# Linear attention and a gated convolution: the output product in 64x64 quadrants, with a new written-out order

## The chip, the core and the metric

The kernel runs on one core of a Trainium2 chip. TensorE (PE; PEld is its weight load) multiplies, VectorE (DVE) and ScalarE (ACT) do the elementwise work and empty the accumulator tiles, GpSimd (POOL) starts the loads, SyncE (SP) starts the stores. The metric is the device time of one execution in microseconds (us); lower is better. Beside the runs there is one profiled execution, whose span goes from its first to its last instruction.

## The reference

For each of 8 batches and 8 heads of dimension 64, over a sequence of 576: `kv = k^T v` (64x64), `out = q kv`, then a root-mean-square norm along the head dimension with a gain. The heads side by side make rows of 512, and these go through a gated convolution layer:

```python
kv = np.einsum('bhsd,bhse->bhde', k, v)
out = np.einsum('bhsd,bhde->bhse', q, kv)
rms = np.sqrt(np.mean(out * out, axis=-1, keepdims=True) + 1e-06)
x = out / rms * g_norm                     # heads side by side: 576 x 512 per batch
h = np.maximum(x @ w_in, 0.0)              # 576 x 1024
conv_out = sum(conv_w[k] * shifted(h, k - 1) for k in range(3))
y = (h * sigmoid(conv_out)) @ w_out        # 576 x 512
```

Inputs and outputs are fp32; the kernel computes in bf16 with fp32 accumulation.

## The kernel before, in words

Everything is unrolled. Small functions (`ops`) each emit a few instructions; the string ORDER lists their calls one after the other, and at the end of the kernel each engine is bound to issue its instructions in exactly that order. A token such as `ot.4.1@1` calls `ot(4, 1)` with accumulator slot 1; `!A` or `!V` gives an eviction to ACT or DVE. There are four accumulator slots in PSUM (`a0` to `a3`, each 128 x 1024 fp32), two buffers each for q, k and v, and four output row buffers.

The names that matter here, with b for the batch and lines of the kernel before:

- `Lq`, `Lk`, `Lv` (lines 310 to 320), `Li`, `Lo`: loads, which cast fp32 to bf16 on the way, all started by POOL in order. A batch's q lies as [128, 4, 576]: a row of partitions holds heads 2w and 2w+1 of slot w in its halves, each with 64 groups of 9 rows. Batch 0's first half comes through a staging tile instead (`pre`, `ca`).
- `qt` (line 372): 36 transposes of 64x64 blocks for two head pairs, `qc` copies them out as `qT`. `kv` (line 344): 36 (or 72) matmuls of 64x64x64 for k^T v. Both use one quarter (quadrant) of the 128x128 array per instruction: `half[v]` chooses the rows, `half[c]` the columns.
- `kvc` (line 355): copies k^T v into `kvbd`, one 128x128 block-diagonal tile per head pair, whose other quarters were zeroed once at the start (lines 260 and 263). Each copy fills one partition half.
- `ot` (line 387): output product of one head pair t; full-width matmuls of 128x128 by 64 and by 512 columns (`mm576`, line 382) with `kvbd` as weights.
- Norm, batches 0 and 1: `sq` (square, ACT), `on` (sums by a matmul with ones), `nl` (reciprocal root, ACT), `mz` (gain and scale, DVE). Batches 2 to 7 in pairs: `sq` and `oc` (copy, both ACT), `ss`, `ln`, `sl`, then `sp` (spreads the scale into PSUM, PE) and `mu` (gain and scale, DVE).
- Layer: `hm` (lines 474 to 481, 288 columns) or `ha`, `hb` (lines 488 to 509, 512 and 128 columns) are x times w_in; `re`, `rea`, `reb` the relu; `ta`, `aa`, `ab` the three taps on DVE; `sg` the sigmoid on ACT; `mg` the product with the gate on DVE; `om` (line 558) times w_out, `ea` empties it, `st` stores.
- `fi` and `fo` (lines 277 to 285): fillers, matmuls of zeros that keep TensorE running while it would wait.

The output product of the kernel before and the copy that feeds it:

```python
    def kvc(b, u, i=None, eng=None):
        if b not in HALF:
            u, i = None, u
        ps = T["kvps", b, u][half[i]]
        to = kvbd[b % 2][half[i], :, half[i]].rearrange("p (u v) e -> p u v e", u=2)
    ...
    def ot(b, t):
        mm576(tl(("ot", b, t), "a", [P, 1024], FP32, "o_ps"), kvbd[b % 2][:, t, :], T["qT", b, t // 2][:, t % 2, :])
```

Of the kernel before, what the change touches and what calls it, by code (L numbers as in the profile page):

```python
# [59 lines left out]
HALF = [0, 1]  # L60
CONV = {0: (0, 1), 1: (1, 1), 2: (2, 2), 3: (4, 2), 4: (6, 1), 5: (7, 1)}
# [18 lines left out]
sg.0.7 fi.1.512@1 fi.1.128@1 qt.3.1@1 hm.1.7.1 hm.1.6.0@2 sg.0.6 qc.3.1!V@4 aa.0.0 re.1.7!A re.0.4!A hm.1.6.1  # L80
hm.1.3.0@1 re.1.6!A ab.0.0 qt.3.0@3 hm.1.2.0@0 hm.1.2.1 mg.0.3 ta.0.4@1 qc.3.0!A@0 sg.0.0 hm.1.3.1 kv.3@2 hm.1.5.0@3
re.1.2!A sg.0.1 ta.0.5 aa.0.2 hm.1.5.1 hm.1.1.0@0 ab.0.2 re.1.3!A kvc.3.0!A mg.0.0 sg.0.4 kvc.3.1!A Lo.1 hm.1.0.0@1
hm.1.0.1 re.1.0!A sg.0.5 ta.1.3@0 hm.1.1.1 ta.1.2 re.1.1!A qt.2.0@2 re.1.5!V qt.2.1@1 Lk.2@1 ot.3.1@3 sq.3.1@0
oc.3.1@4 aa.1.1 Lv.2@1 qc.2.1!V@1 ot.3.0@0 oc.3.0 mg.0.2 ab.1.1 ot.3.3@1 fi.2.128@3 om.0.1.1@3 oc.3.3@0 sq.3.0@1
ta.1.1@1 sg.1.2 ot.3.2@0 Lo.0 sq.3.3@2 sq.3.2@3 qc.2.0!V@2 ta.1.0 aa.1.0 oc.3.2 ab.1.0 hm.1.4.0@2 hm.1.4.1 sg.1.3
Lq.5@0 fi.3.128@1 kv.2@1 om.0.0.1@0 kvc.2.0!V kvc.2.1!V sg.1.0 re.1.4!A ot.2.3@1 mg.1.1 sg.1.1 ta.1.5@0 ot.2.0@2
ta.1.4 sq.2.3@4 oc.2.3@1 oc.2.0@2 sq.2.0@5 mg.1.0 ta.1.7@1 om.0.1.0 ot.2.1@1 aa.1.2 ab.1.2 oc.2.1 om.0.0.0 sq.2.1@6
Lq.4@1 Lv.4@0 sg.1.5 ta.1.6 ea.0.0!A@0 aa.1.3 ot.2.2@2 sg.1.4 ab.1.3 sg.1.7 om.0.3.0@1 sg.1.6 om.0.2.0@0 ea.0.1!V@1
mg.1.2 mg.1.3 sq.2.2@7 Lk.4@0 ss.2@3 ss.3 oc.2.2 ln.1@0 om.0.2.1 Lv.5@1 Lk.5@1 qt.5.1@2 st.0.0 sl.1@0 qt.5.0@3
ea.0.2!A@2 om.0.3.1 sp.3.0.1@0 qc.5.1!V@3 mu.3.0.1@1 sp.2.1.0@2 qc.5.0!A@0 ea.0.3!A@3 mu.2.1.0 kv.4@3 sp.3.0.0@1  # L90
mu.3.0.0 Lq.6@0 kvc.4.0!A kvc.4.1!A qt.4.1@0 qc.4.1!A@4 sp.3.1.1@3 om.0.4.0@2 sp.3.1.0@1 sp.2.0.0@0 st.0.1 mu.3.1.1
mu.3.1.0 qt.4.0@3 om.0.4.1 mu.2.0.0 qc.4.0!A@2 sp.2.1.1@1 ea.0.4!A@0 mu.2.1.1 kv.5@0 kvc.5.1!A sp.2.0.1@3 ot.4.1@1
sq.4.1@4 ot.4.0@2 oc.4.0@3 kvc.5.0!V oc.4.1 Lv.6@0 mu.2.0.1 hb.1.0@0 ha.1.1.0@3 ot.5.0@1 ha.1.1.1 rea.1.1!V@1 sq.4.0@5
reb.1.0!A ot.4.3@2 Lv.7@1 ha.1.0.1@0 ta.2.1@0 oc.5.0@4 Lq.7@1 sq.5.0@6 ot.5.2@1 ha.1.0.0 rea.1.0!V ta.2.0 ot.5.3@3
sq.4.3@7 oc.4.3@0 oc.5.2@1 sq.5.2@0 ha.1.7.0@2 ot.4.2@1 aa.2.0 ha.1.7.1 st.0.4 sq.5.3@1 oc.5.3 sq.4.2@2 oc.4.2
ot.5.1@0 sq.5.1@3 ab.2.0 ha.1.5.0@3 ss.4@1 oc.5.1 ss.5 ln.2@0 hb.1.1@0 rea.1.7!A reb.1.1!A sl.2@1 ha.1.5.1 rea.1.5!A
Lk.6@0 ha.1.4.1@1 ha.1.4.0 sp.5.1.1@2 rea.1.4!A sp.5.0.1@0 sg.2.0 ta.2.5@1 ha.1.2.1@3 mu.5.1.1@0 sp.4.0.1@1 sp.4.1.0@2
mu.5.0.1 mu.4.0.1 ha.1.2.0 mu.4.1.0 ha.1.6.0@0 ta.2.4 sp.4.1.1@1 sp.4.0.0@2 mu.4.1.1 Lk.7@1 mu.4.0.0 rea.1.2!A
ha.1.6.1 rea.1.6!A ha.1.3.1@3 sg.2.1 ha.1.3.0 sp.5.1.0@1 aa.2.2 mu.5.1.0 sp.5.0.0@2 ha.2.0.0@0 mu.5.0.0 qt.6.0@1
rea.1.3!A qc.6.0!A@1 qt.6.1@3 ab.2.2 qc.6.1!A@2 ha.2.5.1@2 ha.2.5.0 mg.2.0 rea.2.5!A@0 ta.2.3@0 ha.2.6.0@1 sg.2.5  # L100
ha.2.0.1 ha.2.6.1 ta.2.2 rea.2.0!A rea.2.6!A aa.2.1 sg.2.4 ha.2.3.0@3 kv.6@2 kvc.6.1!A qt.7.0@0 ab.2.1 hb.2.1@1 sg.2.2
kvc.6.0!A qc.7.0!V@3 ha.2.3.1 reb.2.1!A mg.2.2 sg.2.3 hb.2.0@0 ha.2.7.0@2 ha.2.2.0@1 ta.2.6@1 ta.2.7 rea.2.3!A
ha.2.2.1 reb.2.0!A aa.2.3 kv.7@3 ab.2.3 qt.7.1@0 rea.2.2!A ha.2.7.1 qc.7.1!V@4 kvc.7.1!A rea.2.7!V kvc.7.0!A mg.2.1
ha.2.1.1@1 ot.7.1@3 sg.2.7 sg.2.6 oc.7.1@2 ha.2.4.1@0 ot.7.2@2 sq.7.1@2 ha.2.1.0 rea.2.1!A oc.7.2@0 mg.2.3 ha.2.4.0
ta.3.2@0 om.1.4.0@3 ot.7.3@1 om.1.4.1 ta.3.3 ta.3.7@1 sq.7.2@4 oc.7.3 sq.7.3@5 om.1.1.0@2 aa.3.1 rea.2.4!A ot.6.0@1
ea.1.4!A@1 st.0.2 sq.6.0@7 st.0.3 ab.3.1 ot.6.2@0 ot.7.0@3 st.1.4 ta.3.6 oc.6.2@3 sq.6.2@0 om.1.1.1 sq.7.0@1
om.1.3.0@0 om.1.3.1 sg.3.3 sg.3.2 ea.1.1!V@0 oc.7.0 oc.6.0@1 ot.6.3@2 sq.6.3@3 aa.3.3 ot.6.1@3 oc.6.1 om.1.0.1@1
mg.3.1 sq.6.1@6 ss.6@3 ss.7 ta.3.4@0 om.1.0.0 ln.3@0 ta.3.5 aa.3.2 om.1.2.0@3 ea.1.3!A@2 oc.6.3 ea.1.0!A@3 sl.3@0
sp.6.0.0@0 sp.6.0.1@2 ab.3.2 sp.6.1.1@1 sg.3.5 mu.6.0.1@1 om.1.2.1 sg.3.4 mu.6.0.0 ea.1.2!A@1 sp.6.1.0@2 hm.6.6.0@0
mu.6.1.1 hm.6.1.0@1 mu.6.1.0 hm.6.6.1 sp.7.1.0@2 st.1.3 sp.7.0.0@3 hm.6.1.1 ab.3.3 mu.7.1.0 re.6.6!A@1 hm.6.5.0@0  # L110
hm.6.5.1 re.6.1!A sp.7.0.1@2 sp.7.1.1@1 mu.7.0.0 mg.3.2 mu.7.1.1 re.6.5!A hm.6.0.0@3 mu.7.0.1 ta.3.0@0 hm.6.0.1 sg.3.6
ta.3.1 hm.6.2.0@0 sg.3.7 hm.6.2.1 aa.3.0 re.6.2!A hm.6.4.0@1 hm.6.4.1 re.6.4!A hm.7.3.0@2 hm.7.1.0@0 hm.7.3.1 ab.3.0
hm.7.1.1 hm.7.0.0@1 re.6.0!A re.7.3!A hm.7.0.1 re.7.0!A st.1.1 mg.3.3 hm.6.3.0@3 re.7.1!A hm.6.7.0@2 ta.4.1@1 hm.6.3.1
hm.7.5.0@1 hm.6.7.1 hm.7.4.0@0 ta.4.0 re.6.3!A sg.3.1 hm.7.7.0@3 hm.7.4.1 aa.4.0 hm.7.5.1 ab.4.0 hm.7.7.1 re.6.7!A
sg.3.0 hm.7.2.0@2 hm.7.2.1 re.7.5!A sg.4.1 mg.3.0 om.2.4.1@1 om.2.4.0 sg.4.0 re.7.7!V ta.4.2@0 ta.4.3 ea.2.4!A@2
hm.7.6.0@3 hm.7.6.1 re.7.6!A mg.4.0 om.2.0.1@1 om.2.0.0 re.7.2!A ta.4.6@1 om.2.3.1@3 st.1.2 aa.4.1 ab.4.1 sg.4.3
om.2.3.0 ta.4.7 aa.4.3 sg.4.2 mg.4.1 ab.4.3 sg.4.6 sg.4.7 ta.5.3@0 ta.5.2 aa.5.1 mg.4.3 ta.4.5@1 st.1.0 ea.2.3!A@0
ab.5.1 ta.4.4 aa.4.2 re.7.4!A sg.5.2 sg.5.3 ab.4.2 st.2.3 om.2.1.0@2 om.2.1.1 mg.5.1 om.2.2.0@3 om.2.2.1 om.3.0.0@0
ta.5.0@0 ea.2.0!A@1 sg.4.4 ta.5.1 sg.4.5 om.3.1.0@1 ea.2.1!A@3 mg.4.2 om.3.1.1 aa.5.0 ab.5.0 ea.2.2!A@0 ta.5.6@1
st.2.2 st.2.1 sg.5.0 st.2.0 ta.5.7 om.3.0.1 aa.5.3 sg.5.1 mg.5.0 ta.5.5@0 ab.5.3 ta.5.4 sg.5.7 aa.5.2 ab.5.2  # L120
om.3.4.0@2 sg.5.6 mg.5.3 ea.3.1!A@0 om.3.5.0@3 ea.3.0!V@3 st.3.0 sg.5.4 st.2.4 om.3.3.0@1 st.3.1 sg.5.5 mg.5.2
om.3.2.0@0 om.3.4.1 ea.3.4!A@1 om.3.3.1 st.3.4 om.3.2.1 om.3.5.1 ea.3.2!V@3 st.3.2 ea.3.3!A@2 om.3.6.1@2 st.3.3
ea.3.5!V@0 st.3.5 om.3.6.0 ea.3.6!A@1 st.3.6
"""


@with_exitstack
def kernel(
    ctx: ExitStack,
    tc: tile.TileContext,  # L130
    q: bass.AP,
    k: bass.AP,
    v: bass.AP,
    g_norm: bass.AP,
# [62 lines left out]
    cw = consts.tile([P, NR], FP32, name="cw")  # L197
    g_sb = cw[:, NR - 1:NR]
    sel = consts.tile([P, 4, 32], BF16, name="sel")
    kvbd = [consts.tile([P, NT, P], BF16, name=f"kvbd{i}") for i in range(2)]  # L200
    w_in_sb = consts.tile([P, NT, D_ff], BF16, name="w_in_sb")
    w_out_sb = consts.tile([P, NF, D_model], BF16, name="w_out_sb")
    spread = consts.tile([P, 4, 2, D], BF16, name="spread")
# [423 lines left out]
```

## Time and profile before

| | |
|---|---|
| median of 3 runs | 190.11 us (188.85 to 192.12) |
| profiled execution, its own time | 189.92 us |
| its span | 188.2 us |
| mean granted TensorE clock in it | 0.987 |
| instructions that PE was given in the program | 4,286 |
| moved by DMA | 26.89 MB, mean 143 GB/s |
| k^T v of batch 5 done (PE) | 77.7 us |
| last product with the gate done (DVE) | 178.4 us |

How to read it: busy shares are means over stages with different limits. PE's time includes the fillers. A matmul's duration in a row is its latency, and matmuls overlap, so the distance between starts tells what one costs in a run. The chain of waits follows the last instruction back to what released it; "issue" in it is time in which an engine waited for nothing that the profile shows.

### The profile page before, as it was taken

The numbers are of one execution on the slowest core, as the hardware profiler recorded it, in microseconds if no ns is written. First come the engines' busy times: TensorE is split into PE (matmuls) and PEld (weight loads), VectorE is DVE, ScalarE is ACT, GpSimd is POOL, SyncE is SP. The second block draws the span as 40 slices with busy tenths as digits, with TensorE's granted clock in tenths as the row PEclk, the third lists the DMA queues.
The fourth block names the chain that finished last, engine by engine and source line by source line (L and its number), as shares of the span: only waits on it lengthen the run. The fifth ranks groups of instructions, "written<-read, shape, count | busy, mean of one in ns | idle before, by whom it ended". The sixth has DMA issues, their size and how long they took to land.

```text
span 188.2 us, 4925 instructions
## 1 busy us (share of the span) xinstructions
PE 172.7 (92%) x2108; PEld 93.7 (50%) x2130; DVE 153.9 (82%) x271; ACT 145.6 (77%) x204; POOL 26.9 (14%) x50
## 2 busy tenths in 40 slices
PE   7979998888899993999999999999999999999991
PEld 2444764656454451545335654444467864444440
DVE  3545699998989583469999999998999999999920
ACT  3337499997999981699899999999988874794721
POOL 6964306011330030420000000000000000000000
PEclk9999999999999998799999999999999999999998
DMA  5999999999999999499900000010541000107195
GB/s 210 261 196 204 208 205 208 207 207 209 206 208 209 249 246 168 170 212 207 194 2 3 3 3 3 4 53 0 223 167 61 0 0 3 77 35 273 71 347 202
DMA packets 19417, 26.89 MB, mean 143 GB/s; under 512 B 952, under 2 KB 13508, under 8 KB 19396
## 3 DMA queue, kind: packets, MB, share of 16 engines
q0 software_dynamic: 13616, 15.38, 48.4%
q1 hardware_dynamic: 5776, 11.21, 16.4%
q8 instruction: 16, 0.26, 0.6%
q14 instruction: 5, 0.04, 0.1%
q10 hardware_dynamic: 4, 0.00, 0.0%
HBM read 32.52 MB, written 9.44 MB: 223 GB/s over the span
## 4 chain that ended last, share of the span: by engine, by line
PE 68%; DVE 14%; ACT 8%; issue 5%; DMA 2%; another core or an unknown queue 1%; SPq 0%; ACTq 0%
PE om_ps L565 17%; PE h_ps L492 15%; PE h_ps L479 13%; PE fi_ps L280 7%; PE kv_ps L349 4%; ACT taps L547 3%; DVE h L553 3%; PE qt_ps L376 3%; PE o_ps L384 3%; DVE taps L541 2%; DVE taps L535 2%; PE h_ps L507 2%; DVE taps L529 2%; DVE taps L528 2%; DMA out_dram<-row 2%
## 5 line engine op out<-in xcount | busy, mean ns | idle before, releaser
L565 PE MATMUL om_ps<-w_out_sb,h 128*128 128x512 bf16 x278 | 64.6, 383 | 0.8 <-issue 0.3
L547 ACT ACTIVATE taps<-taps,cw 128x576 bf16<-128x576 bf16 (+1 forms) x48 | 43.1, 935 | 5.9 <-DVE taps L541 5.8
L565 PEld LDWEIGHTS <-h 128*128 128x128 bf16 x288 | 27.7, 98 | 32.5 <-issue 1.2
L225 ACT ACTIVATE h<-h_ps 128x576 bf16<-128x576 f32 (+2 forms) x44 | 31.8, 754 | 6.7 <-PE h_ps L479 6.0
L479 PE MATMUL h_ps<-xT,w_in_sb 128*128 128x288 bf16 x256 | 33.7, 286 | 0.5 <-ACT o L408 0.4
L492 PE MATMUL h_ps<-xT,w_in_sb 128*128 128x512 bf16 x123 | 30.2, 379 | 0.4 <-issue 0.2
L479 PEld LDWEIGHTS <-w_in_sb 128*128 128x128 bf16 x256 | 24.4, 98 | 7.9 <-issue 1.1
L535 DVE TENSOR_TENSOR taps<-taps 128x1152 bf16<-128x1152 bf16 (+1 forms) x24 | 23.0, 959 | 0.5
L541 DVE TENSOR_TENSOR taps<-taps,h 128x1152 bf16<-128x1152 bf16 (+1 forms) x24 | 22.9, 956 | 0.6
L553 DVE TENSOR_TENSOR h<-h,taps 128x1152 bf16<-128x1152 bf16 (+1 forms) x24 | 22.7, 952 | 0.5 <-ACT taps L547 0.5
L393 ACT ACTIVATE sq<-o_ps 128x576 bf16<-128x576 f32 x32 | 20.4, 665 | 2.6 <-PE o_ps L384 2.1
L463 DVE SCALAR_TENSOR_TENSOR xT<-o,cw,sp_ps 128x576 bf16<-128x576 f32 x24 | 18.2, 810 | 5.0 <-PE sp_ps L456 4.9
L528 DVE TENSOR_SCALAR taps<-h,cw 128x576 bf16<-128x576 bf16 (+1 forms) x48 | 20.4, 424 | 1.8 <-ACT h L225 1.7
L219 ACT ACTIVATE row<-om_ps 128x1024 f32<-128x1024 f32 (+1 forms) x17 | 14.8, 869 | 8.3 <-PE om_ps L565 4.9
L529 DVE TENSOR_SCALAR taps<-h,cw 128x576 bf16<-128x576 bf16 (+1 forms) x48 | 20.0, 417 | 0.0
L492 PEld LDWEIGHTS <-w_in_sb 128*128 128x128 bf16 x128 | 11.9, 98 | 12.8 <-issue 0.5
L280 PE MATMUL fi_ps<-zero 128*128 128x512 bf16 (+1 forms) x56 | 14.6, 358 | 2.9 <-DVE zero L262 1.3
L219 ACT ACTIVATE o<-o_ps 128x576 f32<-128x576 f32 x24 | 15.3, 669 | 0.0
L219 ACT ACTIVATE qT<-qt_ps 128x1152 bf16<-128x1152 bf16 x7 | 7.8, 1129 | 6.0 <-PE qt_ps L376 5.9
L214 ACT ACT_TABLE_LOAD x8 | 10.3, 1283 | 2.1 <-issue 2.0
L312 POOL DMA_DIRECT2D q_sb<-in_q_dram x9 | 6.7, 744 | 33.0 <-PE qt_ps L376 31.4
L376 PE MATMUL qt_ps<-ident,q_sb 64*64 64x64 bf16 x576 | 7.5, 196 | 3.4 <-issue 3.0
(73 smaller groups left out, 146.9 us busy)
## 6 DMA issues: line engine op xcount, KB each, us to landing
out_dram<-row SPq DMA_DIRECT2D x14, 512.0 KB, 3.8
k_sb<-in_k_dram POOLq DMA_DIRECT2D x6, 576.0 KB, 13.6
q_sb<-in_q_dram POOLq DMA_DIRECT2D x6, 576.0 KB, 10.9
v_sb<-in_v_dram POOLq DMA_DIRECT2D x6, 576.0 KB, 11.2
out_dram<-row SPq DMA_DIRECT2D x8, 256.0 KB, 2.3
w_in_sb<-in_moe_w_in_dram POOLq DMA_DIRECT2D x4, 256.0 KB, 9.0
w_out_sb<-in_moe_w_out_dram POOLq DMA_DIRECT2D x2, 512.0 KB, 15.5
q_sb<-in_q_dram POOLq DMA_DIRECT2D x3, 288.0 KB, 11.4
```

Source lines behind the costliest of these rows:

```text
L219: nc.scalar.activation(to, fr, AX.Copy)
L225: nc.scalar.activation(to, fr, AX.Relu)
L280: nc.tensor.matmul(ps[:, :cols], zero[:, :P], zero[:, :cols], start=True, stop=True)
L479: nc.tensor.matmul(ps[:, e, :HS], w_in_sb[:, t, f * P:(f + 1) * P], x[:, t, e * HS:(e + 1) * HS], start=(t == 0), stop=(t == NT - 1))
L492: nc.tensor.matmul(ps[:, e], w_in_sb[:, t, f * P:(f + 1) * P], x[:, t, e * 512:(e + 1) * 512], start=(t == 0), stop=(t == NT - 1))
L528: nc.vector.tensor_scalar_mul(tap[:, 0, f % 2, :n, 8:8 + S], h[:, f], cw[:, f:f + 1])
L529: nc.vector.tensor_scalar_mul(tap[:, 1, f % 2, :n, :S], h[:, f], cw[:, 2 * NF + f:2 * NF + f + 1])
L535: nc.vector.tensor_add(tap[:, 1, :, :n, :S], tap[:, 0, :, :n, 7:7 + S], tap[:, 1, :, :n, 1:1 + S])
L541: nc.vector.tensor_add(y, y, h[:, 2 * j:2 * j + 2])
L547: nc.scalar.activation(y, y, AX.Sigmoid, scale=cw[:, NF + f:NF + f + 1])
L553: nc.vector.tensor_mul(h, h, T["tap", c, j][:, 1, :, :n, :S])
L565: nc.tensor.matmul(ps[:, j], h[:, f, m * P:(m + 1) * P], w_out_sb[:, f, :], start=first and f == 4 * i, stop=not first and f == 4 * i + 3)
```

## The change

The heads of a pair no longer share a block-diagonal weight tile. `kv` and `qt` lay the head that comes from rows `half[v]` into columns `half[c ^ v]`, so that for each of the two head pairs the heads lie on both partition halves, crosswise. `kvw` replaces `kvbd`: 64 columns per pair instead of 128, no zeros, filled by one copy of all 128 partitions. `ot(b, i)` computes two head pairs in one call: eight matmuls, each in one quadrant, four with 64 columns and four with 512. It needs two accumulator slots.

Counts in the program: PE 4,592 instructions instead of 4,286. Output product 128 matmuls of 64x64 weights instead of 64 of 128x128. Fillers 8 of 512 columns, 128 of 128 and 20 of 384, instead of 37, 22 and 6. `kvc` 10 copies instead of 20. Evictions: relu of 128x576 23 on ACT and 9 on DVE (before 27 and 5), output rows of 1024 columns 13 and 1 (11 and 3), q^T 8 and 8 (7 and 9).

```diff
-    kvbd = [consts.tile([P, NT, P], BF16, name=f"kvbd{i}") for i in range(2)]
+    kvw = [consts.tile([P, NT, D], BF16, name=f"kvw{i}") for i in range(2)]
...
-        nc.gpsimd.memset(kvbd[1], 0.0)
         pl()
         nc.vector.memset(zero, 0.0)
-        nc.vector.memset(kvbd[0], 0.0)
...
     def kv(b, u=None):
         ps = tl(("kvps", b, u), "a", [P, 2, 512], FP32, "kv_ps")
         for uu in range(2) if u is None else [u]:
-            for r, v, c in quad():
+            for r in range(R):
                 at = slice(r * D, (r + 1) * D)
-                nc.tensor.matmul(
-                    ps[half[c], v, uu * D:(uu + 1) * D],
-                    qkv("k", b)[half[v], 2 * uu + c, at], qkv("v", b)[half[v], 2 * uu + c, at],
-                    start=(r == 0), stop=(r == R - 1))
+                for v in range(2):
+                    for c in range(2):
+                        nc.tensor.matmul(
+                            ps[half[c ^ v], v, uu * D:(uu + 1) * D],
+                            qkv("k", b)[half[v], 2 * uu + c, at], qkv("v", b)[half[v], 2 * uu + c, at],
+                            start=(r == 0), stop=(r == R - 1))
...
-    def kvc(b, u, i=None, eng=None):
-        if b not in HALF:
-            u, i = None, u
-        ps = T["kvps", b, u][half[i]]
-        to = kvbd[b % 2][half[i], :, half[i]].rearrange("p (u v) e -> p u v e", u=2)
-        if u is None:
-            copy(eng, to, ps[:, :, :2 * D].rearrange("p v (u e) -> p u v e", u=2))
-        else:
-            copy(eng, to[:, u], ps[:, :, u * D:(u + 1) * D])
+    def kvc(b, u=None, eng=None):
+        uu = slice(0, 2) if u is None else slice(u, u + 1)
+        copy(eng, kvw[b % 2].rearrange("p (u v) e -> p u v e", u=2)[:, uu],
+             T["kvps", b, u][:, :, :P].rearrange("p v (u e) -> p u v e", u=2)[:, uu])
...
     def qt(b, u):
-        for r, v, c in quad():
+        for r in range(R):
             at = slice(r * D, (r + 1) * D)
-            nc.tensor.transpose(ps[half[c], v, at], qkv("q", b)[half[v], 2 * u + c, at], ident[half[v], half[v]])
+            for v in range(2):
+                for c in range(2):
+                    nc.tensor.transpose(
+                        ps[half[c ^ v], v, at], q_sb[half[v], 2 * u + c, at], ident[half[v], half[v]])
...
-    def ot(b, t):
-        mm576(tl(("ot", b, t), "a", [P, 1024], FP32, "o_ps"), kvbd[b % 2][:, t, :], T["qT", b, t // 2][:, t % 2, :])
+    def ot(b, i):
+        u, vs = (i, (0, 1)) if b in JOINT else (i // 2, (i % 2,))
+        for v in vs:
+            tl(("ot", b, 2 * u + v), "a", [P, 1024], FP32, "o_ps")
+        for at in (slice(512, S), slice(0, 512)):
+            for c in range(2):
+                for v in vs:
+                    nc.tensor.matmul(
+                        T["ot", b, 2 * u + v][half[c], at], kvw[b % 2][half[c ^ v], 2 * u + v, :],
+                        T["qT", b, u][half[c ^ v], v, at], start=True, stop=True)
```

JOINT lists all eight batches. Two new functions (`cd`, `cp`) and a branch in `sg` are not reached from the new ORDER. ORDER is new from end to end. Two places of it that the prediction speaks of, the second half of batch 0 and the stretch with batch 4's and 5's k^T v:

```diff
-ot.0.0@0 pc ot.0.1@2 sq.0.0@0 on.0.0@1 qc.0.1!V@1 nl.0.0@0 mz.0.0@0 Lk.0.1 fi.3.512@3 kv.0.1@3 kvc.0.1.1!V sq.0.1@1
-fi.2.128@1 on.0.1@1 nl.0.1 Li.0.1 Li.0.0 Li.1.0 kvc.0.1.0!V fi.1.512@0 fi.2.128@0 ot.0.3@0 mz.0.1 sq.0.3@2 ot.0.2@3
+fi.4.128@2 fi.3.128@2 qt.0.1@2 sq.0.1@1 fi.8.128@1 fi.1.128@1 on.0.1@1 qc.0.1!V@1 Lv.0.1 nl.0.1 Li.0.0 Li.0.1 kv.0.1@3
+kvc.0.1!V fi.2.128@2 ot.0.1@2,3 sq.0.3@2 sq.0.2@3 pn Li.1.1 mz.0.1 fi.16.128@1 on.0.3@1 Li.1.0 Lq.1.0@1 fi.4.128@0
...
-mu.3.0.0 Lq.6@0 kvc.4.0!A kvc.4.1!A qt.4.1@0 qc.4.1!A@4 sp.3.1.1@3 om.0.4.0@2 sp.3.1.0@1 sp.2.0.0@0 st.0.1 mu.3.1.1
-mu.3.1.0 qt.4.0@3 om.0.4.1 mu.2.0.0 qc.4.0!A@2 sp.2.1.1@1 ea.0.4!A@0 mu.2.1.1 kv.5@0 kvc.5.1!A sp.2.0.1@3 ot.4.1@1
+ss.3 om.0.2.1@0 ln.1@0 ea.0.0!A@1 qc.4.0!V@2 om.0.2.0 ea.0.2!A@2 sl.1@0 qt.5.0@1 sp.2.0.0@3 mu.2.0.0@1 sp.3.1.1@2
+Lk.4@0 mu.3.1.1 kv.4@0 Lv.5@1 qc.5.0!A@0 sp.3.0.1@3 kvc.4!A sp.2.1.1@1 mu.3.0.1 sp.3.0.0@2 mu.2.1.1 mu.3.0.0
+om.0.3.0@0 ot.4.1@3,1 sq.4.3@4 oc.4.3@3 oc.4.2 sp.3.1.0@2 om.0.3.1 sq.4.2@5 Lk.5@1 sp.2.0.1@1 ea.0.3!A@3 mu.3.1.0
+mu.2.0.1 sp.2.1.0@2 kv.5@3 ot.4.0@1,0 kvc.5!A hb.1.0@3 mu.2.1.0 oc.4.1@0 Lq.6@1 sq.4.1@6 sq.4.0@7 ha.1.0.0@2
```

## The prediction

> **What bounds the kernel now.** I read the page first, its busy shares and its slices. TensorE is 92% busy, and the slice near 71 us is the only one after the start in which all of PE, DVE and ACT fall and the granted clock falls behind it.
>
> ```profile
> PE 172.7 (92%) x2108; PEld 93.7 (50%) x2130; DVE 153.9 (82%) x271; ACT 145.6 (77%) x204; POOL 26.9 (14%) x50
> ```
>
> Then the chain of waits in order of time, around that slice (start, us, what). The reader is to see that the chain lies on PE before and after, and that in between PE stands in the middle of one run of 36 transposes, waiting for nothing that the profile shows. A smaller stand of the same kind lies at 41 us, in the middle of a run of k^T v products.
>
> ```profile
> 41.18 0.93 issue
> ...
> 70.71 0.28 PE qt_ps L376 x17
> 70.99 2.99 issue
> 73.97 0.41 PE qt_ps L376 x18
> ```
>
> Counted in the program's order, the two stands come before PE's instructions 1,220 and 2,244: 1,024 apart. The DMA view of the long stand names a queue of kind "instruction", and it moves one piece inside it; the page has 16 such pieces, 0.26 MB, for 4,286 PE instructions. So PE's code comes in pieces of about 256 instructions, and at these two borders (each 256k - 60) the next piece was late.
>
> ```profile
> q0 software_dynamic: 532, 0.59, 116.6%
> q8 instruction: 1, 0.02, 2.0%
> ```
>
> Next the stages around it (length, busy time of PE, PEld, DVE, ACT, POOL, granted clock, DMA share, GB/s). During the stand nothing else fills the time; for the 3.5 us after it the clock is 0.52.
>
> ```profile
> 71.00:74.00 3.00, 0.03 (x4) 0.02 (x4) 1.25 (x2) 0.00 (x0) 0.00 (x0) 1.00 1.18 202
> 74.00:77.50 3.50, 3.50 (x97) 1.80 (x96) 0.81 (x1) 1.73 (x2) 0.00 (x0) 0.52 0.16 28
> ```
>
> Behind 77.7 us (end of the k^T v products of batch 5) PE is 98 to 99% busy in every stage up to 178.4 us, DVE 70 to 99%; the chain runs on PE to 136 us and on DVE from 151 us. So what stands before 77.7 us shifts the end one for one, and PE work that is added behind it counts in full.
>
> **The change part by part**, against the profiled execution: span 188.2, its own time 189.92 (1.7 around the span), 0.2 under the median 190.11.
>
> *Output product (ot).* Before, each 128-row tile costs a 64-column and a 512-column matmul. The starts lie 0.216 apart for 512 columns (the 22 h_ps of line 492 take 4.91 us, 0.223) and 0.028 for 64: 0.49 for two tiles. After, eight 64x64 matmuls do two tiles. Do four quadrants run side by side? The k^T v rows say yes:
>
> ```profile
> 104.68 0.38 PE L492 MATMUL h_ps<-xT,w_in_sb 128*128 128x512 bf16 x1
> 104.99 0.78 PE L349 MATMUL kv_ps<-v_sb,k_sb 64*64 64x64 bf16 x72
> 105.58 0.51 PE L376 MATMUL qt_ps<-ident,q_sb 64*64 64x64 bf16 x36
> 106.03 0.45 PE L507 MATMUL h_ps<-xT,w_in_sb 128*128 128x128 bf16 x5
> ```
>
> 72 of them start within 0.59 us, 8.2 ns each, 33 ns for four: the price of one of 64 columns. So two tiles cost 0.033 + 0.216 = 0.25. But the same rows price the way in and out. From the last 512-column matmul to the first quadrant 0.31 instead of 0.22: 0.09. From the first of 36 transposes to the next full-width matmul 0.45, where 36 at 8.2 ns are 0.30: 0.15. Together 0.24 per round trip, and nearly every one of the 16 new ot stands alone between full-width work (two follow a k^T v directly). 0.25 + 0.24 = 0.49: I cost the product at nothing. The ends: all trips hidden, 16 x 0.24 = -3.8, of which the seven behind batch 5's k^T v reach the end, -1.7; two quadrants at a time instead of four, 16 x 0.25 = +4.0.
>
> The Trainium skill has this as a rule that speaks against the change: TensorEngine Tiling (Array Packing), Key Properties, says that changing the tiling mode drains TensorE. The rows above agree, with 0.09 and 0.15 us. By the page's theoretical speedup alone, without the drain, the sum would be up to 3.8 us lower.
>
> *k^T v eviction (kvc).* 20 half-partition copies become 10 of all 128 partitions and the same columns. Rows: ACT 9 x 377 and 3 x 271 ns, DVE 3 x 420 and 5 x 288. After: ACT 4 and 2, DVE 2 and 2: ACT -2.2 us, DVE -1.3. If twice the partitions took twice the time it would be 0; the DVE cast of 128x288 at 309 ns says they don't. Neither engine is last where these stand, so nothing at the end. Zeroing of the two padded tiles goes: DVE 0.27, and on POOL 0.55 that stands ahead of all loads (it ran at 2.29, the next one began at 2.75). POOL's loads start 0.46 earlier: -0.5, since DMA is at 205 to 209 GB/s from 20 to 60 us and the start waits on landings. Ends 0 and -1.5 (the new order also takes fewer steps from the second half's k^T v to the first h_ps, now at 18.5).
>
> *Evictions that change engine.* DVE gains 4 relu (753 ns), one small one (about 0.69) and loses two output rows (1,223) and a q^T (752): +0.5; ACT about 0. Hidden: DVE has 20 us idle before 77.7.
>
> *Fillers.* 37 x 512, 22 x 128 and 6 x 384 columns become 8, 128 and 20: 10.2 us to 12.1 at 0.216, 0.056 and 0.162 a piece. All but two stand ahead of batch 3's output product, where PE waits for ACT, DVE and loads. Cover gone: +1.9.
>
> *Code pieces.* The old stands cost 2.99 + 0.93, and the slow clock 3.5 x 0.48 = 1.7: -5.6 together. What is late next? The last k of batch 5, issued at 53.5, landed at 69.7 (the longest, 16.2); batch 5's k^T v would come at 76.5 - 4.7 = 71.8, so 2.1 us of room. In the new order I counted PE's work between borders. At the old stands PE took 6.4 us (67.6 to 74.0) and 5.8 (36.3 to 42.1) from one border to the next, wait included; so a piece must last about 6 us while loads run. The old order had 2.3 us of PE work in the piece that stood for 3 us. The new one's poorest is 2,244 to 2,500 (rest of a transpose, k^T v of batch 4, five sp, half an om, one ot): 3.4 us of PE work, but its sp wait for five mu, 5 x 0.81 = 4.1, plus 0.5 before the first: 4.6. It lacks between 0 (asked for early enough) and 1.8 (6.4 - 4.6); I take the middle, +0.9. Pieces 964 to 1,220 (3.9 of PE, but 7.5 of ACT) and 3,012 to 3,268 (4.9, DVE 5.6) should last.
>
> *What moves behind batch 5's k^T v.* om.0.4 (8 matmuls, 1.8) now comes behind it; seven new ot against sixteen old ones give 3.4 instead of 3.9, one sp 0.1 less: +1.1 of PE work, charged in full. DVE loses 0.9 there: no credit, since PE is the bound up to 136 us. SP's stores and POOL's loads keep number and size; batch 6's v goes behind 7's, but PE needs 7 first now. The tail has 24 to 28 om matmuls behind the last product with the gate, as now: 9.8 us, unchanged.
>
> Sum: 189.9 - 5.6 + 0.9 - 0.5 + 1.1 = **185.8**, from 0 for ot, kvc and fillers.
>
> **The rivals.**
> *The stand comes back.* The new piece 2,244 to 2,500 is the densest, and loads still run then. With the old 2.99 and the slow clock 1.7 in place of 0.9: 189.6. For it: 3.4 us of work. Against: the mu waits stretch it, and they stretch it whether or not code is late.
> *Slower: two accumulator tiles at once.* The new ot needs two of the four PSUM tiles free at the same moment and holds both until ACT's square and copy, 4 x 0.67. If each of the 16 waits for one more ACT eviction (128x576, 0.65), that is +10.4: 196.2. It cancels the gain at 0.26 each and makes the kernel slower by 2% at 0.5 each. For it: ACT is 98% busy from 50 to 60 and over 99% from 100 to 120 us. Against: h_ps of line 492 takes 8 x 0.216 = 1.7 to fill and 1.02 to evict, so two tiles carry it meanwhile.
> *More gain.* The drains behind batch 5 hidden (-1.7) and the start 1.5 earlier instead of 0.5: 185.8 - 2.7 = 183.1, to 182 without the 0.9.
> *The stand is no late code.* Then it and the slow clock stay wherever they come from: 185.8 + 4.7 = 190.5. The piece that lands inside it speaks against. The Trainium skill speaks for it: Runtime: NRT & Kernel Launch, Instruction fetch mechanics, calls the cost of crossing a 16 KiB block mostly hidden. The trace disagrees, with 2.99 us at such a border.
> *Only two quadrants at a time at 512 columns,* which is the change not doing what it says: +4.0, 189.8. The 33 ns for four of 64 columns speak against.
>
> **How the numbers follow.** Forecast 41 in 100 (own range 183.8 to 187.8), stand back 18, more gain 15, two tiles 14, no late code 6, two quadrants 6. Two per cent, about what this kernel's measurement can tell, is 186.3 and 193.9. Faster by more: 28 of the 41, the 15, and 3 of the stand's: 46. Slower by more: 12 of the two tiles' and 3 elsewhere: 15. The rest, 39. The range 182.5 to 191.0 leaves out the two-tile case and the low end of the more-gain case, 19.
>
> **What would show it.** No "issue" piece over 1 us in the chain between 60 and 80 us and no clock of 0.5 there; the k^T v of batch 5 over by 72 to 74 us; runs of four o_ps quadrants with 512 columns each starting within about 0.02 us, and about 0.33 from there to the next full-width matmul; the first h_ps before 18.5; from batch 5's k^T v to the end about 111.6 (now 110.5). An "issue" piece at instruction 2,500 is the first rival; PE waiting on ACT's square, copy or relu before o_ps the second. I am wrong if PE is no longer the last wait between 78 and 136 us.

## The result, and the profile after

| | kernel before | changed kernel |
|---|---|---|
| median | 190.56 us, 20 runs (188.79 to 192.34) | 188.06 us, 20 runs (186.94 to 190.32) |
| profiled execution: own time, span | 189.92, 188.2 | 186.94, 185.2 |
| first h_ps | 18.50 | 18.35 |
| k^T v of batch 5 done | 77.7 | 74.4 |
| from there to the end of the span | 110.5 | 110.8 |
| last matmul | 183.95 | 181.14 |

The ratio is 0.988, 95% interval 0.985 to 0.991: 1.2% faster, which by the 2% bound counts as the same. The forecast was 185.8, 2.3% faster.

The page of the changed kernel. PE is again the busiest engine, and its granted clock (one digit for each fortieth of the span, 9 for nine tenths or more) never falls:

```profile
PE 171.3 (93%) x2263; PEld 97.1 (52%) x2285; DVE 151.9 (82%) x268; ACT 142.1 (77%) x196; POOL 26.7 (14%) x49
...
PEclk9999999999999999999999999999999999999999
```

Stages (length, busy time of PE, PEld, DVE, ACT, POOL, granted clock, DMA share, GB/s). Where the kernel before stood for 3 us and then ran at a clock of 0.52, the changed one works at full clock. But in 33 to 36.5 us PE is busy for 1.97 of 3.50 us, while DVE and ACT are busy throughout:

```profile
33.00:36.50 3.50, 1.97 (x80) 1.27 (x79) 3.50 (x8) 3.48 (x5) 2.07 (x3) 1.00 1.21 209
...
72.00:77.50 5.50, 5.30 (x119) 3.03 (x119) 2.47 (x4) 5.32 (x10) 1.48 (x2) 1.00 1.17 224
```

The chain of waits puts that hole down to DVE, where a product into h ends last:

```profile
35.67 0.68 DVE h L586
36.35 0.12 issue
36.47 0.20 PE on_ps L382
```

It is not DVE. The timeline of PE shows the hole between a run of 36 transposes and a matmul that sums squares (start, duration, engine, line, what, count):

```profile
34.60 0.48 PE L372 MATMUL qt_ps<-ident,q_sb 64*64 64x64 bf16 x36
36.47 0.20 PE L382 MATMUL on_ps<-sq,ones 128*128 128x64 bf16 x1 [1.39 <-DVE h L586]
```

By ORDER that matmul needs accumulator slot 2, which DVE's copy of q^T frees. The timeline of DVE in the changed kernel has the copy first and the product into h well behind it:

```profile
34.38 0.74 DVE L219 COPY qT<-qt_ps 128x1152 bf16<-128x1152 bf16 x1
...
35.60 0.75 DVE L586 TENSOR_TENSOR h<-h,taps 128x1152 bf16<-128x1152 bf16 x1
```

The timeline of PE at the same place in a kernel that differs only in its first fillers (e11 below):

```profile
34.24 0.48 PE L372 MATMUL qt_ps<-ident,q_sb 64*64 64x64 bf16 x36
34.80 0.19 PE L382 MATMUL on_ps<-sq,ones 128*128 128x64 bf16 x1
```

And that of DVE in e11:

```profile
34.01 0.74 DVE L219 COPY qT<-qt_ps 128x1152 bf16<-128x1152 bf16 x1
...
35.23 0.74 DVE L586 TENSOR_TENSOR h<-h,taps 128x1152 bf16<-128x1152 bf16 x1
```

In e11 the matmul starts 0.05 after the copy (34.75), long before DVE begins the product into h. In the changed kernel the copy ends at 35.12 and PE stands 1.35 us more. Counted in the program, PE stands there at its instruction 1,217 (256 x 5 - 63; the prediction's count is three too high, and its 1,220 and 2,244 are 1,217 and 2,241). The DMA view of 34 to 36.5 us has one piece of queue q8 in it, the queue whose 16 pieces fitted PE's 4,286 instructions in the kernel before, and a smaller one of another queue:

```profile
q0 software_dynamic: 448, 0.50, 117.9%
q8 instruction: 1, 0.02, 2.2%
q14 instruction: 1, 0.01, 0.8%
```

So the long stand, at instruction 2,241, is gone with its slow clock, and the one at 1,217 has grown from 0.93 to 1.35 us.

The output product, in the chain of the changed kernel (start, us, what):

```profile
96.79 1.46 PE om_ps L598 x6
98.25 0.37 PE o_ps L393 x8
98.62 0.54 PE h_ps L499 x2
```

The trace gives the eight starts of this product to the nanosecond: 0, 3, 6, 10 for 64 columns, then 52, 55, 59, 62 for 512, and the next full-width matmul at 374. The four quadrants do run side by side.

### The profile page after: what moved, and what is told of

It reads as the page before. It is cut to its first block, busy times and chain, and to the rows that moved or that the text cites. A ratio compares the mean times of both kernels' runs of the same rounds, so it can differ in the third digit from the quotient of the medians.

```text
span 185.2 us, 5220 instructions
## 1 busy us (share of the span) xinstructions
PE 171.3 (93%) x2263; PEld 97.1 (52%) x2285; DVE 151.9 (82%) x268; ACT 142.1 (77%) x196; POOL 26.7 (14%) x49
## 4 chain that ended last, share of the span: by engine, by line
PE 67%; ACT 14%; DVE 11%; DMA 3%; issue 2%; SPq 0%; ACTq 0%
PE om_ps L598 23%; PE h_ps L499 14%; PE h_ps L486 14%; PE fi_ps L276 4%; DMA stg<-in_v_dram 3%; DVE xT L470 3%; PE o_ps L393 3%; PE kv_ps L347 3%; ACT o L217 3%; ACT sq L400 3%; ACT taps L580 2%; ACT o L415 2%; ACT h L223 2%; ACT L212 2%; PE h_ps L514 2%
## 5 line engine op out<-in xcount | busy, mean ns | idle before, releaser
L598 PE MATMUL om_ps<-w_out_sb,h 128*128 128x512 bf16 x279 | 63.9, 379 | 0.8 <-issue 0.2
L223 ACT ACTIVATE h<-h_ps 128x576 bf16<-128x576 f32 (+2 forms) x39 | 29.1, 778 | 3.7 <-PE h_ps L486 3.3
L499 PE MATMUL h_ps<-xT,w_in_sb 128*128 128x512 bf16 x122 | 29.2, 379 | 0.5 <-issue 0.2
L217 ACT ACTIVATE row<-om_ps 128x1024 f32<-128x1024 f32 (+1 forms) x19 | 16.8, 894 | 9.3 <-DMA out_dram<-row 5.7
L217 ACT ACTIVATE o<-o_ps 128x576 f32<-128x576 f32 x24 | 15.8, 674 | 0.2 <-PE o_ps L393 0.2
L276 PE MATMUL fi_ps<-zero 128*128 128x128 bf16 (+1 forms) x135 | 14.0, 248 | 1.9 <-DVE zero L259 1.3
L225 DVE TENSOR_SCALAR h<-h_ps 128x576 bf16<-128x576 f32 (+2 forms) x13 | 11.1, 855 | 3.8 <-PE h_ps L499 1.5
L276 PEld LDWEIGHTS <-zero 128*128 128x128 bf16 x136 | 9.9, 109 | 4.0 <-issue 1.4
## 6 DMA issues: line engine op xcount, KB each, us to landing
q_sb<-in_q_dram POOLq DMA_DIRECT2D x6, 576.0 KB, 10.9
```

What stands on the lines that cost most here:

```text
L217: nc.scalar.activation(to, fr, AX.Copy)
L223: nc.scalar.activation(to, fr, AX.Relu)
L276: nc.tensor.matmul(ps[:, :cols], zero[:, :P], zero[:, :cols], start=True, stop=True)
L499: nc.tensor.matmul(ps[:, e], w_in_sb[:, t, f * P:(f + 1) * P], x[:, t, e * 512:(e + 1) * 512], start=(t == 0), stop=(t == NT - 1))
L598: nc.tensor.matmul(ps[:, j], h[:, f, m * P:(m + 1) * P], w_out_sb[:, f, :], start=first and f == 4 * i, stop=not first and f == 4 * i + 3)
```

## The experiments

Ratios are against the kernel before in the same rounds (its medians there: 189.7 to 190.5).

| run | median us (runs) | ratio, 95% interval |
|---|---|---|
| e1_borders_later | 186.12 (6) | 0.979, 0.975 to 0.983 |
| e2_borders_earlier | 186.06 (6) | 0.979, 0.974 to 0.983 |
| e11_borders_78_later | 185.83 (6) | 0.977, 0.973 to 0.982 |
| e4_two_quadrants | 188.05 (6) | 0.987, 0.984 to 0.991 |
| e6_full_width_product | 186.85 (6) | 0.983, 0.979 to 0.987 |
| e7_zeroing_back | 186.00 (6) | 0.979, 0.975 to 0.983 |
| e13_before_borders_moved | 186.75 (6) | 0.984, 0.980 to 0.989 |
| e14_before_borders_moved_one_copy | 186.55 (6) | 0.983, 0.979 to 0.986 |
| e12_before_one_copy | 189.83 (12) | 0.998, 0.994 to 1.001 |
| e3_new_order_old_product | 189.96 (12) | 0.997, 0.994 to 1.000 |
| e15_new_order_old_product_54_later | 189.17 (12) | 0.998, 0.995 to 1.001 |
| e5_half_copies | 189.44 (12) | 0.998, 0.995 to 1.001 |
| e17_idle_second_copy | 189.66 (12) | 0.998, 0.995 to 1.001 |
| e10_half_copies_two_engines | 193.78 (6) | 1.017, 1.010 to 1.024 |
| e16_half_copies_side_by_side | 193.14 (6) | 1.016, 1.011 to 1.021 |
| e8_before_30_more | 193.21 (6) | 1.015, 1.010 to 1.020 |
| e9_before_30_more_warm | 193.19 (6), 188.42 to 193.98 | no interval |

### Where the code borders lie

Theory: PE stands where a numbered piece of its code comes late, so moving the numbers moves the stand. Rival: what stands is data or another engine. Fillers of the same length in fewer or more instructions move every later border (e1, e2, e11: 30 fewer, 42 more, 78 fewer).

```diff
 e1
-fi.36.128@0
+fi.5.512@0 fi.16.128@0
 e2
-fi.7.512@1
+fi.28.128@1
 e11
-fi.36.128@0 ... fi.16.128@1
+fi.9.512@0 ... fi.4.512@1
```

> The changed kernel with the first filler call written as 5 x 512 and 16 x 128 columns instead of 36 x 128: 30 PE instructions fewer at the very start, the same filler time, nothing else. Every border between pieces of code falls 30 instructions later in the work. Theory (late code pieces still cost the changed kernel time): the 1.5 us stand before PE instruction 1,217 at 36.5 us goes, because the piece that ends there now has the waits of the norm inside it; 1.2 to 1.6 us faster than the changed kernel, 186.5 to 187. Rival (the stand at 36.5 us is the wait for VectorE's product that the view names): the stand stays and the time is that of the changed kernel, 188.1 within 0.5.

> The changed kernel with the second filler call as 28 x 128 instead of 7 x 512 columns: 42 PE instructions more before the first k^T v, the same filler time. Borders fall 42 instructions earlier in the work. Theory: counted in the changed kernel's trace, the pieces that end near 48 us and near 61 us then get less than the 6 us that a piece takes, by about 0.8 and 2.3 us, and the one at 36.5 us is relieved of 1.4: stands at new places, 1 to 2.5 us slower than the changed kernel, 189 to 190.5. Rival (borders mean nothing): 188.1 within 0.5, the stand at 36.5 us stays.

> The changed kernel with the same filler time at its start in 78 fewer TensorE instructions (36 of 128 columns become 9 of 512, and 16 of 128 become 4 of 512). Theory (with every code piece asked for some 6 us ahead of need, the sum of the stands is least near 80 instructions later): no stand above 0.7 us, granted clock above 0.995 in nearly all runs, 185.4 to 186.2. Rival (the shift only moves the loss): 187 to 188.

All three are 1.9 to 2.2 us under the changed kernel, and the stand at 36 us is gone in each. e2 had been expected to be slower. Of the two new stands that were named, the one at 61 us came with 0.27 us, the one at 48 didn't, and another of 0.49 came at 67, on a border as well: the requirement of 6 us per piece is an upper estimate. The three kernels also vary less: 185.2 to 187.3 over 18 runs, against 186.9 to 190.3. The granted clock tells a part of it: its mean is 0.991 or less in 8 of the changed kernel's 20 runs (their median is 189.3), in all 17 runs of the kernel before that stood beside e1 and e2, and in 1 of these 18. But the other twelve of the 20 spread from 186.9 to 188.9 too, around 187.9. The profiled execution was the fastest of all, 1.1 us under the median; why the others are slower at the same clock is open, since none of them was profiled.

The same was tried on the kernel before: 30 more instructions early (e8), the same further back (e9), and 202 more for the same columns, placed so that no piece is short by much (e13).

```diff
 e8
-fi.9.512@0
+fi.4.512@0 fi.20.128@0
 e9
-fi.12.512@2
+fi.7.512@2 fi.20.128@2
 e13: 23 fillers of 512 columns as 92 of 128, and in ot
+        ps, kt, q_sb = tl(("ot", b, t), "a", [P, 1024], FP32, "o_ps"), kvbd[b % 2][:, t, :], T["qT", b, t // 2][:, t % 2, :]
+        step = {0: 256, 1: 256, 2: 128, 3: 128}.get(b, 512)
+        for at in [slice(512, S)] + [slice(x, min(x + step, 512)) for x in range(0, 512, step)]:
+            nc.tensor.matmul(ps[:, at], kt, q_sb[:, at], start=True, stop=True)
```

> The kernel before with nine filler matmuls of 512 columns at its start put as 4 of 512 and 20 of 128: the same filler time, 30 more instructions on TensorE ahead of all else, so every code border comes 30 instructions earlier in the work. Theory (stands belong to numbered instructions: a piece is asked for at the border before and needs some 6 us under load): the stand of 2.99 us at 71 us becomes 1.2 to 1.6 us and starts near 69.6, that near 41 us stays at about 0.9 to 1.3, a new one of up to 1.9 us comes near 45; with the long stand gone the granted clock is above 0.995; 189.5 to 190.8 in all. Rival (the long stand belongs to data that are late in the work at that place): a stand of about 3 us stays at 71, clock 0.987, 190.5.

> As e8_before_30_more, which was spoiled at its start (512-column fillers still took 0.427 us each up to 10.7 us there, in the kernel before up to 7.2 us), with the 30 more instructions put behind that: five of the twelve filler matmuls of 512 columns ahead of the first k^T v become 20 of 128. Theory (stands belong to numbered instructions): stands end at instructions 1,217 (near 41 us, 1.0 to 1.3), 1,473 (near 46 us, 1.5 to 1.9; none there in the kernel before) and 2,241 (near 71 us, 1.2 to 2.7); k^T v of batch 5 ends within 1.2 us of 77.7, and the time is 190 to 192. Rival (e8 lost by the stands and not by its start): 193, within 1.

> The kernel before with 202 more TensorE instructions at no more columns: 23 filler matmuls of 512 columns between 6 and 18 us as 92 of 128, and the 512-column part of each product of q with k^T v in two pieces (batches 0 and 1) or four (batches 2 and 3). By a requirement of 6 us from border to border the stands near 41 and 71 us go and four of 0.3 to 0.7 us are left. Theory (the prediction's term: 5.6 us of the kernel before are its two stands and the slow clock behind them): clock above 0.995, k^T v of batch 5 over 2.5 to 4 us earlier than 77.7, 185 to 187. Rival (a stand also lets VectorE and ScalarE catch up, so that much of its length comes back elsewhere): the stands gone and yet 187.5 to 189. Second rival (the pieces still come late at other places): 190, within 1.

In e8's trace the stand at instruction 1,217 is 1.04 us long and a new one at 1,473 1.68, as expected; but the one at 2,241 is still 2.48 us instead of 1.2 to 1.6. Its start was cold (last section), so its time, 193.21 at a mean clock of 0.967 to 0.986 where 189.5 to 190.8 and over 0.995 had been forecast, can't be put to the stands alone. e9's chain has the first two stands where they were expected, and the one at 2,241, expected with 1.2 to 2.7, is gone:

```profile
40.87 0.43 PE kv_ps L349 x39
41.30 0.98 issue
42.29 0.47 PE kv_ps L349 x33
...
45.80 0.72 PE qt_ps L376 x70
46.52 1.62 issue
48.14 0.22 PE qt_ps L376 x2
```

Its time misses the theory's 190 to 192: four runs at 193.2 to 194.0, with a mean clock of 0.975 to 0.980, lie where the rival put them (193), and two at 188.4 and 189.8 lie below both. Why the four are slow is open: the profile is of the run at 189.8. In it the clock behind the second stand is low as well:

```profile
50.00:56.00 6.00, 5.89 (x96) 3.15 (x96) 4.02 (x8) 4.67 (x9) 0.88 (x2) 0.72 1.20 205
```

e13 gained 3.0 us from moved borders, with the same columns of work for PE. In its chain two shorter stands are left, at instructions 2,241 and 2,497:

```profile
67.15 0.41 PE kv_ps L349 x36
67.56 0.86 issue
68.41 0.51 PE kv_ps L349 x36
...
72.90 0.22 PE kv_ps L349 x2
73.11 0.71 issue
73.83 0.80 PE kv_ps L349 x70
```

That is 1.57 us of stands and a clock of 0.997, instead of 3.92 us, and 1.7 us lost to the slow clock; its first h_ps is 0.54 later. 5.6 - 1.6 - 0.5 = 3.5 us should have been won, and the profiled executions differ by 189.92 - 186.88 = 3.0. So the price of the stands was about right, and the rival (much of it comes back elsewhere) falls.

### Product, copies, order, zeroing

e3 and e15 have the functions of the kernel before in the new order; e4 the new product one tile at a time (`JOINT = []`). e6, built on e2, takes eight full-width matmuls for two tiles; e7, also on e2, puts both zeroings back.

```diff
 e6
+        wide = kvw[b % 2][:, 2 * u:2 * u + 2, :].rearrange("p v e -> p (v e)")
+        for v in vs:
+            for at in (slice(544, S), slice(512, 544), slice(256, 512), slice(0, 256)):
+                nc.tensor.matmul(T["ot", b, 2 * u + v][:, at], wide, T["qT", b, u][:, v, at], start=True, stop=True)
 e7
+        nc.gpsimd.memset(kvbd[1], 0.0)
         pl()
         nc.vector.memset(zero, 0.0)
+        nc.vector.memset(kvbd[0], 0.0)
```

> The new order with the old functions: block-diagonal weights with their zeroing, two half copies of each k^T v on the engine that the new order names, full-width output products, each pair's two tiles one right behind the other. 32 filler instructions are added before the first k^T v, so that the border at 36.5 us falls where the changed kernel has it. Theory (the order alone carries the gain; the quadrant product costs what the old one did, 0.47 against 0.49 us for two tiles): the changed kernel's time within 0.8 us, slower rather than faster for 3.4 us of ACT and VectorE copies and 0.5 us later loads: 188 to 189. Rival (the quadrants halve the product and carry the gain): 3 to 4 us of PE come back, 191 to 192.

> e3_new_order_old_product (new order, old product and copies; 189.96 us with one stand of 0.85) with 86 fewer TensorE instructions at the start and the same filler time, so that no stand above 0.3 us is expected. Theory (what e5_half_copies and e6_full_width_product cost adds up: 3.4 and 0.6 on 186.0): 189.4 to 190.2, the stand at 36 us gone and nothing won by it. Rival (copies and stand are lost in the same place): 188 to 189.

> The changed kernel with JOINT empty: the same instructions, but each of a pair's two tiles by itself, so that only two quadrants work at a time, the second tile right behind the first. Theory (four quadrants run side by side at 512 columns too): two tiles take 0.25 us more, 4 us over the kernel, of which the seven pairs behind batch 5's k^T v reach the end: 1.5 to 2.5 us slower than the changed kernel, 189.5 to 190.5. Rival (PSUM or the read ports let only two run at full rate anyway): the changed kernel's time within 0.5.

> The kernel of e2_borders_earlier with the eight quadrant matmuls of q with k^T v put as eight full-width ones (two tiles, columns in pieces of 32, 32, 256, 256; k^T v of two tiles taken side by side as a 128x128 weight, so the numbers that come out are not those of the reference); the count of instructions, the copies and the order stay. Theory now (the prediction's step: 0.49 against 0.49 us for two tiles, worth nothing): 186.1, within 0.4, and k^T v of batch 5 to the last matmul 106.7, within 0.2. Rival (the quadrants themselves carry what e3_new_order_old_product lost): 186.9 to 188.

> The kernel of e2_borders_earlier with the two zeroings of the before kernel put back (128x512 bf16 on GpSimd ahead of its loads, 128x512 on VectorE among its first work) on tiles that nothing reads. The prediction's step: loads start 0.46 later and everything behind them 0.4 to 0.5 later: 186.5 to 186.6. Theory now (the trace of the changed kernel shows the first half of v landing later although its load was issued earlier, and the first h_ps only 0.15 earlier): 186.1, within 0.25.

e4 could not tell two quadrants from four: the trace has its starts at 0, 3, 13, 17 and 52, 56, 66, 69 ns, so the tiles still overlapped. e6 lies 0.85 us over e7 of the same rounds, over its theory's 186.5 and just short of the rival's 186.9; from batch 5's k^T v to the last matmul it took 107.1, against 106.8 in e2. But its pieces of 32 and 256 columns cost 0.54 us for two tiles in the trace, more than the 0.49 of the old product, and 16 x (0.54 - 0.47) = 1.1 us: e6 pays for its own pieces. The quadrants are worth little. e7 equals e2: the zeroing cost nothing. e3 and e15 are no better than the kernel before, with a stand at 36 us and without: the new order by itself wins nothing (e3 missed both its forecasts). Beside e13, the old order with moved borders in the same rounds, e15 is even 2.4 us slower, 189.17 against 186.75.

Fewer copies of k^T v are what the new order lives on. e5 makes them in halves again; e12 and e14 make one copy in the old order, the second without its long stands.

```diff
 e5, on e2
+        for i in range(2):
+            copy(eng, kvw[b % 2][half[i]].rearrange("p (u v) e -> p u v e", u=2)[:, uu],
+                 T["kvps", b, u][half[i]][:, :, :P].rearrange("p v (u e) -> p u v e", u=2)[:, uu])
 e12, on before; e14 the same on e13
+        copy(eng, kvw[b % 2].rearrange("p (u v) e -> p u v e", u=2)[:, uu],
+             T["kvps", b, u][:, :, :P].rearrange("p v (u e) -> p u v e", u=2)[:, uu])
```

> The kernel of e2_borders_earlier (186.06 us) with each copy of k^T v to SBUF made as two copies of half the partitions on the same engine, as the kernel before made them; TensorE's instructions are the same, so code pieces fall where they did. Theory now: these copies stand between k^T v and its product with q, and the two halves one behind the other are most of what e3_new_order_old_product lost against the changed kernel; each costs the path about 0.2 us where the copy is the last thing that the product waits for: 186.9 to 187.8. Rival (the prediction's own step: hidden under other work): 186.1, within 0.3.

> The kernel before, its order and its count of TensorE instructions, with the two half copies of each k^T v made one copy of all partitions (at the first one's place, on its engine), and the product with q taken full-width with two tiles of k^T v side by side as weight (numbers other than the reference's). Theory now (a copy's length goes to the path, as e5_half_copies showed in the new order): each of the ten batches' or halves' copies gives 0.3 us back where nothing else is awaited: 187.5 to 189 beside 190.1 of the kernel before. Rival (the prediction's step: in the old order the second half is hidden under other work): 190.1, within 0.5.

> e13_before_borders_moved with one copy of each k^T v and the full-width product of e12_before_one_copy (numbers other than the reference's). Beside e12 (0.5 us gained on the kernel before) it says whether the copies are hidden in the old order or only behind its stands. Theory now (the stands hid them): 2 to 3 us below e13_before_borders_moved. Rival (the old order hides them by the work that it puts behind them): within 0.7 of e13_before_borders_moved.

In the new order ten more copies cost 3.4 us (e5 against e7, same rounds), nearly their own length, 10 x 0.35, and more than either forecast allowed. In the old order ten fewer give 0.5 (e12) and 0.2 (e14), both within their intervals: there most of them is hidden, as the prediction had it, and not by the long stands. In e14's profile the stand at 2,497 is 1.48 us instead of e13's 0.71, so up to 0.6 more may have been won and lost again on a border.

Why do they cost so much? Either the product waits longer for them, or they take time from VectorE and ScalarE. e10 gave one half to each engine, e16 the same with two tiles as targets, e17 left the product with one copy and put a second one behind it that nothing reads.

```diff
 e10, e16
-            copy(eng, ...
+            copy("VA"[i], ...
 e17, on e2, behind the one copy
+        copy(eng, spare[eng][half[1]].rearrange("p (u v) e -> p u v e", u=2)[:, uu],
+             T["kvps", b, u][half[1]][:, :, :P].rearrange("p v (u e) -> p u v e", u=2)[:, uu])
```

> As e5_half_copies (189.44 us) with the two half copies side by side, one on VectorE and one on ScalarE, so that the wait between k^T v and its product is that of one copy again while each engine has ten copies. Theory now (it is the time between k^T v and the product that goes to the path): 186.0 to 187. Rival (it is the two engines' own time, both nearly always busy): 188 to 189.5.

> e10_half_copies_two_engines again, with the two halves of k^T v in two tiles: there ScalarE's copy waited for VectorE's, 7.0 us over 5 waits, since both wrote one tile, so they were not side by side. Now only k^T v itself is awaited by both. Theory (the time between k^T v and the product goes to the path): 186 to 187.3, beside 186.06 with one copy and 189.44 with two on one engine. Rival (two queues that both stand until k^T v is done lose what they ran ahead): 188.5 to 191.

> The kernel of e2_borders_earlier (186.06 us) with its one copy of k^T v and behind it, on the same engine, a second copy of one partition half into a tile that nothing reads. The engines' time and the accumulator's hold are those of e5_half_copies (189.44), but the product with q waits for the first copy alone. Theory (the time between k^T v and the product goes to the path): 186.0 to 187. Rival (the engines' own time, what stands behind the copy in their queues): 188.5 to 189.5.

e17 speaks for the engines' own time: 189.66 although the product waits no longer than in e2. It shares with e5 that the accumulator is held longer, so the time alone doesn't tell these two apart; at one place the trace does. In e2 the copy of q^T that PE waits for ends at 46.07 us. In PE's timeline of e2 the matmuls of line 486 wait for it:

```profile
46.13 1.14 PE L486 MATMUL h_ps<-xT,w_in_sb 128*128 128x288 bf16 x8 [0.60 <-DVE qT L219]
```

In e17 VectorE makes the second copy of k^T v (0.43) ahead of that copy of q^T, which ends at 47.32, and in PE's timeline of e17 the wait is 0.74 us longer:

```profile
47.37 0.90 PE L489 MATMUL h_ps<-xT,w_in_sb 128*128 128x288 bf16 x6 [1.34 <-DVE qT L220]
```

The rest of the 3.4 us wasn't followed from place to place. From 30 to 60 us ScalarE is busy for 29.70 us and VectorE for 29.29 in e2:

```profile
30.00:60.00 30.00, 28.74 (x610) 17.70 (x608) 29.29 (x59) 29.70 (x46) 7.42 (x10) 1.00 1.21 203
```

In e13 it is 29.08 and 28.95. That this difference is why the old order hides a second copy is argued, not shown. e10 and e16 missed all their forecasts and did not do what they were made for. In VectorE's timeline of e16 its half stands behind eight small operations of its queue, although k^T v was done at 9.36:

```profile
10.99 0.28 DVE L219 CAST kvw<-kv_ps 64x128 bf16<-64x128 f32 x1
```

In ScalarE's timeline the other half still begins when VectorE's ends:

```profile
11.36 0.27 ACT L217 ACTIVATE kvw<-kv_ps 64x128 bf16<-64x128 f32 x1 [4.29 <-DVE kvw L219]
```

What holds it is the program: as built, ScalarE's copy waits for the semaphore count that VectorE's copy raises, with two target tiles as with one. Why the build orders two copies out of one accumulator is open. PE stands for 1.14 us there, its clock falls behind it, and the second half's k^T v comes 2.9 us later than in e2: the first 3 of e16's 7 us.

## Why the prediction fell short, by its own steps

- *Code pieces, -5.6:* this is the step that failed, and in one clause: "Pieces 964 to 1,220 ... should last". I had counted on 7.5 us of ACT work to stretch that piece. PE didn't wait for it: it came from one border to the next in 4.5 us without the stand (30.6 to 35.1), and stood 1.35. The 0.93 credited for that stand was not earned, it costs 1.35 now, and slow clocks stayed in 8 of 20 runs. The size of the term was about right: e13 won 3.0 where 3.5 was due. Take the stand away by moving borders, and the changed kernel runs at 186.12, 186.06 and 185.83: the forecast of 185.8 is that of the kernel without it, in part by luck, since the terms below miss both ways.
- *The piece 2,244 to 2,500, +0.9:* PE passes the border at 2,497 (70.72 us) without a stand; the largest gap in that piece, 0.54 between starts ahead of batch 4's k^T v, is a wait for ACT in the profile. The rival "the stand comes back" came true in part, at the border at 1,217.
- *Start, -0.5:* wrong. POOL's first load was issued at 4.37 instead of 4.82, yet the first half of v landed at 7.97 instead of 7.47, and the first h_ps came 0.15 earlier; the zeroing put back (e7) costs nothing.
- *ot at nothing:* right to about 0.02 us a product. The way in costs 0.093, and 0.374 passes from the first quadrant to the next full-width matmul: 0.47 for two tiles against 0.49. The drain that the Trainium skill names (TensorEngine Tiling (Array Packing), Key Properties) shows as 0.09 in and about 0.10 out. The rivals "two quadrants" and "more gain" fall.
- *kvc and fillers at nothing:* for kvc about right in the old order (e12, e14); no run takes the fillers by themselves. What I missed is the other side: the new order has no room for a second copy (e5, 3.4).
- *Two accumulator tiles at once:* the chain runs over ACT's evictions of the two tiles at 71.3 to 73.6 and 80.3 to 83.5 us, but PE is busy for 5.30 of 5.50 us around the first: there, and too small.
- *Behind batch 5's k^T v, +1.1:* 110.8 against 110.5, +0.3, so this term was 0.8 too large. The first half brought 3.3 of the 5.2 us expected, and of the 1.9 missing the stand is 1.35 and the start 0.35, the piece at 2,500 gives 0.9 back, and 1.1 isn't assigned. All this is the profiled execution, 186.94; the median of 188.06 lies another 1.1 us higher, and that is open too.
- *"The stand is no late code":* falls. Moving borders alone moves stands, in both kernels. The Trainium skill (Runtime: NRT & Kernel Launch, Instruction fetch mechanics) calls crossing a 16 KiB block mostly hidden; here e13 won 3.0 us from where the crossings lie.

So most of the 2.5 us comes from where PE's instruction numbers fall, and not from the product. With moved borders the old kernel is at 186.75 with 1.57 us of stands left, about 185.2 by subtraction (an estimate from e13's chain), and the new one at 185.83 to 186.12. The new order costs time (e15) and its single copies win it back (e5); together with the product, no gain of their own was seen here.

## What to carry to other kernels

In an unrolled kernel with dense runs of small matmuls, count PE's instructions: a change that adds or removes some ahead of a dense run moves every later code border, and can win or lose 2 to 3 us that have nothing to do with it. Before judging such a change, shift the borders of both kernels by splitting a filler, and compare the best of each. A stand on a border can be put down to whatever engine last finished something; a kernel with shifted borders shows whether that engine was really waited for.

## What the runs showed of the hardware

- While loads run, a piece of 256 PE instructions can need about 6 us: the stands of 0.9 us and more in the kernel before, the changed one, e8, e9 and e14 end 5.8 to 6.4 us after PE passed the border before. PE goes on 1.3 to 1.6 us after the DMA of the piece is done: 35.06 to 36.47 in the changed kernel, 40.56 to 42.11 and 72.64 to 73.97 in the kernel before. It isn't a fixed price: e9 passes from 1,985 to 2,241 in 3.7 us without a stand. There the code of the next piece began to move at 70.14, as PE reached 1,985; in the kernel before it began at 71.66, 4.1 us after PE had. What sets that moment is open.
- Short stands can bring the granted clock to half: 3.5 us at 0.52 behind 2.99 us, 6 us at 0.72 behind 0.98 and 1.62 (e9), and in e16 2 us at 0.50 (the stages of its trace) behind stands of 1.33 and 1.14. They need not: behind 1.35 us in the profile of the changed kernel and 1.48 in e14's it stays at 1.00.

```profile
13.00:15.00 2.00, 1.94 (x16) 1.40 (x15) 0.00 (x0) 0.20 (x1) 1.22 (x2) 0.50 1.12 208
```

- TensorE's speed at the start varies from run to run. In the kernel before, fillers of 512 columns take 0.427 us each up to 5.4 us and 0.216 from about 7 us; in e8, and in e12, whose fillers are those of the kernel before, they take 0.427 up to 10.9 and 10.6 us, and the first k^T v comes 2.4 and 2.1 us later. The trace's record of the granted clock begins only at 5.8, 10.9 and 10.6 us, so the 1.00 of a stage before that says nothing. PE's timeline in the kernel before, fillers ahead of the first k^T v:

```profile
6.81 3.09 PE L280 MATMUL fi_ps<-zero 128*128 128x512 bf16 x13
```

The same in e8:

```profile
7.50 4.76 PE L280 MATMUL fi_ps<-zero 128*128 128x512 bf16 x14
```

The Trainium skill (TensorE: Matmul & The Clock Gate, Part 1: The HAM clock gate) says that the warm-up's length varies between runs with the phase of a free-running window. That it varies, e12 beside the kernel before agrees; that the phase does it, no run here shows.
- A copy of 64 partitions takes as long as one of 128 with the same columns: 0.375 and 0.378 us on ACT for 256 columns.
